# New instruction orders for a fused linear-attention and mixture-of-experts kernel: loads, first-batch slots, attention steps, GpSimd sums, layer-2 products

## Chip, cores, metric

The kernel runs on one core of one Trainium2 chip. The metric is the device time of one execution in microseconds (us). Each experiment was timed in five rounds beside the kernel before, on one of three chips, so runs are compared by their ratio to the kernel before of the same call. Traces are one execution each.

## The reference

Linear attention over 8 batches (8 heads, 576 tokens, head size 64) gives rows of 512 numbers. Four experts, each two layers without routing, work on every row and are summed with normalised weights:

```python
def phi(x):
    return np.where(x > 0, x, np.exp(x) - 1.0) + 1.0
q_p, k_p = phi(q), phi(k)
kv = np.einsum('bhsd,bhse->bhde', k_p, v)
z = np.sum(k_p, axis=2)
out = np.einsum('bhsd,bhde->bhse', q_p, kv) / (np.einsum('bhsd,bhd->bhs', q_p, z)[..., None] + 1e-06)
# rows x: (4608, 512); 4 experts, w1: (512, 1024), w2: (1024, 512)
for e in range(E):
    h = np.maximum(x @ w1[e], 0.0)
    y += p[:, e:e + 1] * (h @ w2[e])
```

## The kernel before

The rows are worked on in nine batches of 512 (the ninth collects 64 left-over rows of each of the eight). From the second batch on, both layers use a seven-product scheme in place of eight: half-size blocks P1 to P7, with sums of weights (DVE, once), of tokens (GpSimd) and of h (GpSimd) prepared ahead. One batch with one expert is a *unit*, 14 slots long; 32 units make up most of the time.

Everything hangs on order. Each piece of work is put at a position (a number), all pieces are sorted by position, and each engine then gets its instructions in that order:

```python
work.sort(key=lambda w: w[0:2])
for _, _, g in work:
    g[0](*g[1:])
```

Waits between engines follow from the data and the buffers and are set by the framework. So a position cannot make the result wrong; it decides what an engine stands behind. These are the parts (cuts marked with `...`):

```python
    def layer2_product(j, e, hT, hss, p, i):
        ...
            run, side = pys[i][:, 0:DH], pys[i][:, DH:Dm]    # two halves of one tile in PSUM
        ...
        for k in range(FH):
            nc.tensor.matmul(out=ps, lhsT=lhsT(k), rhs=rhs[:, k], ...)   # L666
        ...
        add_acc(j, e, ns, ps, ds, first and e == 0)          # DVE reads the half (L568); ACT if it is the first and e == 0

    class Block:                      # layer 1 of one unit, half of the rows of h
        # at +0 p1, +3 p2, +5 p6, +8 p7, +9 p5, +9.1 c22, +11 p4, +13 p3
        def p3(self):
            x = xT_of(self.j)
            self.products(self.e5, lambda k: s_block(self.e, 2, k), x[:, 2:4, NH:NT])   # L731
            add_relu(self.h[:, :, 0, NH:NT], self.e5, self.u2)                          # DVE, L715

        ...
            order = L2ORD ...         # (2, 5, 1, 6, 3, 7, 4)
            for m in range(14):
                put_at(at + L2AT[m], layer2_product, j, e, h, hss, order[m // 2], m % 2)
```

P1, P6, P7 and P4 of layer 2 run through the same PSUM half (`run`), one after the other, and DVE adds the half to the output after each. P6 can't start before DVE has read what P1 left.

`DMA` in the configuration is the order in which GpSimd issues the loads of the weights (`w210`: layer 2, expert 1, first half) and of batch 1's parts (`k0`, `v1`, `lk0`). `L2P`, `WS1`, `WS2`, `TS0`, `L1P`, `BLK` and the first `ATTN` entry place the work of the first batch, during which everything is loaded; the second `ATTN` entry, `HSUM`, `L2AT`, `TSUM` place the work of every later batch.

## Time and profile before

| | before |
|---|---|
| time, median of 4 rounds | 507.53 us (506.90 to 507.89) |
| span of the profiled run | 507.7 us |
| first layer-1 matmul of the experts | 18.63 us |
| last matmul, then tail | 502.2 us, then 5.5 us |
| bare stream time of all 4,343 matmuls (columns / 2.4 ns, the slope measured below) | 464.5 us |

From the page of the profile (section 1: busy time by engine; section 2: busy tenths and granted TensorE clock in 40 slices of 12.7 us; section 4: the chain that ended last, by engine):

```profile
span 507.7 us, 11592 instructions
PE 489.3 (96%) x4343; PEld 409.3 (81%) x4343; DVE 377.4 (74%) x800; ACT 337.4 (66%) x680; POOL 357.9 (70%) x339
...
PE   8987989999999999999999999999999999999995
PEld 3445656688888888888888888888888888888884
...
PEclk9999989999999999999999999999999999999999
DMA  8999952653345234442345234523231020002002
...
PE 81%; DMA 7%; DVE 3%; ACT 3%; issue 2%; SPq 1%; POOL 1%; DVEq 0%; POOLq 0%
```

For holes this text uses a finer reading. In this trace a matmul of 256 columns is followed by the next start after 109 ns, one of 512 columns after 216 ns, one of 130 columns after 57 ns (medians); eight of 256 columns take 0.87 us. Columns / 2.4 ns + 2.5 ns, a fit to these medians, gives all three and is taken for every matmul; what passes beyond that is a *hole*. Summed in this way (worked out from the trace's starts):

| stretch, us | 18.4 to 60 | 60 to 80 | 80 to 100 | 100 to 130 | 130 to 480 |
|---|---|---|---|---|---|
| holes before, us | 6.63 | 5.03 | 1.89 | 0.87 | 4.91 |

What TensorE waited for between 18 and 100 us (the waits view, longest in total first: us, times, longest):

```profile
PE py L577 <- DMA w<-in_moe_w_dram: 1.9, 1, 1.9
PE pb L731 <- ACT u L742: 1.9, 4, 0.9
PE pe L731 <- DMA w<-in_moe_w_dram: 1.0, 1, 1.0
PE pb L731 <- DVE s L605: 0.8, 1, 0.8
```

The timeline of TensorE at these loads (start, length, ..., in brackets the idle time before it and its releaser):

```profile
29.66 1.89 PE L577 MATMUL py<-w,h 128*128 128x512 f16 x8 [1.89 <-DMA w<-in_moe_w_dram]
...
43.49 0.61 PE L731 MATMUL pe<-xT,w 128*128 128x256 f16 x4 [0.99 <-DMA w<-in_moe_w_dram]
44.94 0.61 PE L731 MATMUL pb<-tt,s 128*128 128x256 f16 x4 [0.84 <-DVE s L605]
```

The first waits for half of expert 0's w2, the second for half of expert 2's w1, the third for a sum of that w1.

The timeline at the start of a later batch, P1 (`py<-w,h`), a product of layer 1, P1's second half, then P6 (`py<-t,hs`):

```profile
298.00 0.60 PE L666 MATMUL py<-w,h 128*128 128x256 f16 x4
298.44 0.60 PE L731 MATMUL pb<-xT,w 128*128 128x256 f16 x4
298.87 0.60 PE L666 MATMUL py<-w,h 128*128 128x256 f16 x4
299.69 0.60 PE L666 MATMUL py<-t,hs 128*128 128x256 f16 x4 [0.22 <-DVE acc L568]
```

From 298.87 to 299.69 are 0.82 us where 0.44 are needed: a hole of 0.38 us. The bracket says 0.22, because the profile models a matmul's end some 0.16 us past the next possible start (groups follow each other after 0.44 us and are shown 0.60 long). Between 130 and 480 us it shows of before:

```profile
PE py L666 <- DVE acc L568: 1.1, 5, 0.2
PE psum_nd L463 <- DMA qT<-qp: 0.3, 1, 0.3
```

### The profile page before, as it was taken

Reading aid. Unit: us, or ns where it says so; the run is one execution under the profiler, and the core shown is the slowest. Engines: PE = TensorE matmul, PEld = TensorE weight load, DVE = VectorE, ACT = ScalarE, POOL = GpSimd, SP = SyncE. Lnnn points to the kernel's source line nnn. Section 1 sums busy time; section 2 is a strip of 40 time slices with the busy share of each in tenths; the row PEclk is TensorE's granted clock in tenths of the full one; section 3 lists DMA queues with packets and bytes.
Section 4 is the critical chain, followed back from the end, with each engine's and each line's share of the span. In section 5 each row is a group of like instructions: output and inputs, shape, how many; then the busy total and the mean of one; then the engine's idle time right before and its main releaser. Section 6 shows DMA issues by size and latency. Waiting matters only on the chain.

```text
span 507.7 us, 11592 instructions
## 1 busy us (share of the span) xinstructions
PE 489.3 (96%) x4343; PEld 409.3 (81%) x4343; DVE 377.4 (74%) x800; ACT 337.4 (66%) x680; POOL 357.9 (70%) x339
## 2 busy tenths in 40 slices
PE   8987989999999999999999999999999999999995
PEld 3445656688888888888888888888888888888884
DVE  5546878879876987688868886878688756775675
ACT  5756968984889478946895689558954465446530
POOL 4744304687967796779777977697669877987773
PEclk9999989999999999999999999999999999999999
DMA  8999952653345234442345234523231020002002
GB/s 242 199 225 218 281 137 81 222 119 66 99 135 150 65 81 145 149 87 79 125 146 109 60 125 151 113 48 107 84 67 33 8 95 1 1 1 85 1 1 84
DMA packets 81880, 53.65 MB, mean 106 GB/s; under 512 B 46176, under 2 KB 75360, under 8 KB 81824
## 3 DMA queue, kind: packets, MB, share of 16 engines
q1 hardware_dynamic: 71520, 41.12, 28.7%
q0 software_dynamic: 9824, 11.27, 11.9%
q8 instruction: 34, 0.56, 0.4%
q10 hardware_dynamic: 480, 0.52, 0.3%
q14 instruction: 22, 0.18, 0.1%
HBM read 45.16 MB, written 9.44 MB: 108 GB/s over the span
## 4 chain that ended last, share of the span: by engine, by line
PE 81%; DMA 7%; DVE 3%; ACT 3%; issue 2%; SPq 1%; POOL 1%; DVEq 0%; POOLq 0%
PE py L666 36%; PE pb L731 22%; PE pe L731 16%; DMA w<-in_moe_w_dram 5%; PE py L577 3%; DVE acc L568 2%; PE psum_nd L463 1%; DMA rawb<-in_k_dram 1%; DMA qT<-qp 1%; PE psum_kv L423 1%; SPq L274 1%; ACT psum_ee L314 1%; PE pe L666 1%; SPq L252 1%; PE pb L666 0%
## 5 line engine op out<-in xcount | busy, mean ns | idle before, releaser
L568 DVE SCALAR_TENSOR_TENSOR acc<-py,p_sb,acc 128x256 f32<-128x256 f32 (+1 forms) x382 | 180.4, 488 | 53.0 <-PE py L666 47.1
L715 DVE CUSTOM_DVE_ANT_0 h<-pe,u 128x512 f16<-128x512 f32 x140 | 96.5, 689 | 44.0 <-PE pe L731 24.4
L731 PEld LDWEIGHTS <-w 128*128 128x128 f16 x1120 | 108.3, 98 | 21.8 <-issue 3.4
L633 POOL TENSOR_TENSOR hs<-h 128x512 f16<-128x512 f16 x64 | 73.8, 1153 | 65.1 <-DVE h L715 57.3
L666 PEld LDWEIGHTS <-h 128*128 128x128 f16 x1024 | 100.2, 98 | 13.3 <-issue 1.3
L666 PE MATMUL py<-w,h 128*128 128x256 f16 x744 | 106.4, 273 | 0.1
L742 ACT COPY u<-pb 128x512 f32<-128x512 f32 x140 | 82.4, 589 | 34.4 <-PE pb L731 32.4
L731 PEld LDWEIGHTS <-s 128*128 128x128 f16 x840 | 82.2, 98 | 13.4 <-DVE s L605 1.5
L635 POOL TENSOR_TENSOR hs<-hs,h 128x512 f16<-128x512 f16 x64 | 74.7, 1167 | 18.6 <-PE py L666 16.0
L731 PE MATMUL pb<-tt,w 128*128 128x256 f16 x560 | 84.0, 273 | 1.9 <-ACT u L742 1.9
L666 PEld LDWEIGHTS <-hs 128*128 128x128 f16 x768 | 73.8, 97 | 13.4 <-issue 3.1
L639 POOL TENSOR_TENSOR hs<-h,hs 128x512 f16<-128x512 f16 x64 | 74.4, 1162 | 6.4 <-PE py L666 5.4
L666 PE MATMUL py<-t,hs 128*128 128x256 f16 x496 | 74.3, 272 | 1.7 <-DVE acc L568 1.7
L637 POOL TENSOR_TENSOR h<-h 128x512 f16<-128x512 f16 x64 | 74.4, 1162 | 0.0
L757 ACT ACTIVATE h<-pe 128x512 f16<-128x512 f32 x70 | 41.7, 596 | 49.1 <-PE pe L731 47.9
L751 ACT COPY pe<-pb 128x512 f32<-128x512 f32 x70 | 40.6, 580 | 46.8 <-PE pb L731 45.2
L775 ACT ACTIVATE h<-pb 128x512 f16<-128x512 f32 x70 | 41.6, 595 | 3.5 <-PE pb L731 3.2
L731 PE MATMUL pb<-tt,s 128*128 128x256 f16 x280 | 42.0, 273 | 1.0 <-DVE s L605 0.8
L731 PE MATMUL pe<-tt,s 128*128 128x256 f16 x280 | 42.5, 275 | 0.0
L731 PE MATMUL pe<-xT,w 128*128 128x256 f16 x248 | 37.2, 273 | 1.0 <-DMA w<-in_moe_w_dram 1.0
L731 PE MATMUL pb<-xT,w 128*128 128x256 f16 x248 | 37.2, 272 | 0.4 <-ACT h L775 0.3
L577 PE MATMUL py<-w,h 128*128 128x512 f16 x128 | 35.0, 384 | 2.3 <-DMA w<-in_moe_w_dram 1.9
(120 smaller groups left out, 607.9 us busy)
## 6 DMA issues: line engine op xcount, KB each, us to landing
out_dram<-acc SPq DMA_DIRECT2D x32, 256.0 KB, 2.5
w<-in_moe_w_dram POOLq DMA_DIRECT2D x14, 512.0 KB, 10.8
rawb<-in_v_dram SPq DMA_DIRECT2D x26, 256.0 KB, 2.7
rawb<-in_q_dram SPq DMA_DIRECT2D x26, 256.0 KB, 2.9
rawb<-in_k_dram SPq DMA_DIRECT2D x26, 256.0 KB, 2.8
w<-in_moe_w_dram POOLq DMA_DIRECT2D x4, 256.0 KB, 7.5
rawb<-in_k_dram POOLq DMA_DIRECT2D x4, 256.0 KB, 10.6
rl<-in_q_dram SPq DMA_DIRECT2D x16, 64.0 KB, 2.4
```

The lines of the kernel that those rows point to most:

```text
L568: nc.vector.scalar_tensor_tensor(out=acc, in0=ps, scalar=pscal, in1=acc, op0=AO.mult, op1=AO.add)
L577: nc.tensor.matmul(out=py, lhsT=rows(hT, fj)[:, ns * P : (ns + 1) * P], rhs=w2_sb[e][:, fj, :], start=(fj == 0), stop=(fj == FC - 1),)
L633: nc.gpsimd.tensor_tensor(out=hs[0], in0=a21, in1=a22, op=AO.add)
L635: nc.gpsimd.tensor_tensor(out=hs[1], in0=hs[0], in1=a11, op=AO.subtract)
L637: nc.gpsimd.tensor_tensor(out=a21, in0=a11, in1=a21, op=AO.subtract)
L639: nc.gpsimd.tensor_tensor(out=hs[3], in0=a12, in1=hs[1], op=AO.subtract)
L666: nc.tensor.matmul(out=ps, lhsT=lhsT(k), rhs=rhs[:, k], start=first and k == 0, stop=k == FH - 1, skip_group_check=True,)
L715: nc.vector._custom_dve(TENSOR_ADD_SAT, out=out, in0=ps, in1=u, s0=BIG, s1=0.0)
L731: nc.tensor.matmul(out=ps[:, kk], lhsT=lk(kc), rhs=rhs[:, kc], start=first and kk == 0 and kc == 0, stop=kc == 1, skip_group_check=True,)
L742: nc.scalar.copy(u, self.b)
L757: nc.scalar.activation(self.h[:, :, 0, 0:NH], self.e5, AF.Relu)
L775: nc.scalar.activation(self.h[:, :, 1, 0:NH], self.b, AF.Relu)
```

## The change

Its intent: a new order on every engine, so that weights come when they are needed, batch 1's attention holds TensorE up less, and DVE and GpSimd finish before TensorE needs them. No instruction is added or removed. The core of the diff (long lines cut with `...`; `L1P`, `L2P`, `TS0`, `WS1`, `WS2`, `TSUM1`, `PR` and the first `ATTN` entry change in the same way):

```diff
-    "DMA": (..., 'w200', 'w110', 'w201', 'w111', 'w211', 'lk1', 'lv1', 'lk0', 'k0', 'lv0', 'w210', 'w120', 'w121', 'w221', 'v0', 'w220', 'v1', 'k1', 'w130', 'w131', ...),
+    "DMA": (..., 'w201', 'w200', 'w110', 'w111', 'lk1', 'w120', 'lk0', 'w210', 'w121', 'v1', 'w211', 'v0', 'k0', 'w130', 'lv1', 'w131', 'k1', 'k2', 'v2', 'lv0', ...),
-    "BLK": (-4.0, 3.0, 13.0, 20.0, 28.0, 35.0, 53.0),
+    "BLK": (0.5, 7.5, 16.0, 23.0, 31.0, 38.0, 56.0),
 ...
         dict(
-            v=(0.2, 6.3, 8.4, 9.7),
-            k=(1.3, 2.7, 5.7, 11.5),
-            kd=(7.1, 4.3, 10.8, 15.3),
-            lv=13.3,
+            v=(4.4, 8.7, 12.1, 14.8),
+            k=(0.3, 2.9, 6.7, 11.25),
+            kd=(7.1, 3.84, 14.3, 14.8),
+            lv=10.36,
 ...
-    "HSUM": ((-6.3, -5.5, -4.6, -4.4), (1.5, 2.7, 5.4, 7.2)),
+    "HSUM": ((-5.2, -3.9, -3.7, -1.3), (0.3, 2.7, 2.7, 5.7)),
-    "L2AT": (3.7, 3.8, 5.4, 6.6, 7.1, 8.3, 9.0, 10.0, 12.1, 12.5, 13.3, 14.1, 16.5, 16.7),
+    "L2AT": (3.9, 5.0, 5.8, 7.0, 7.2, 8.4, 9.1, 10.3, 12.9, 13.1, 15.1, 15.1, 16.8, 16.8),
-    "TSUM": (-7.4, -1.8, -1.8, 0.0),
+    "TSUM": (-6.7, -4.7, -1.6, -0.7),
```

## The prediction

> **What bounds the kernel now.** 507.37 us. TensorE is the wall: the page gives it 96% busy, the chain of waits 81%. In the timeline eight 256-column matmuls take 0.87 us, 109 ns each[...]. The rest is start (layer 1 begins at 18.6 us), end (last matmul 502.2, then 5.4 us) and holes. From start to start, holes beyond that rate are about 13 us between 18.6 and 100 us and 5 us later: nearly only one of 0.38 us per batch (143, 195, 247, 299, 351 us), layer 2's product waiting for a DVE accumulation, and 0.46 us at 374 us for the transposed q. The change alters orders only, so it can only close or open holes.

> **What moves, costed.**

> 1. Load order. From 15 to 68 us the DMA engines are saturated (share 1.0 to 1.4 in the windows); a weight half lands every 2.5 us, a part of q or k every 0.85, of v 0.67, a left piece 0.3. Before, TensorE waits 2.06 us at 27.4 for half of expert 0's w2 (landed 29.62), and 1.16 and 1.01 us at 42 to 45 for expert 2's w1 (landed 43.44) and its sums. Adding up the new order (estimates): expert 0's w2 complete at 27.1, expert 1's w1 unchanged at 32.05, expert 2's at 40.2, expert 3's at 50.1 (was 55.5), q3 at 62.4. The hole at 27.4 mostly moves: 1.2 us at 31 for expert 1's w1, and 0.6 us because a sum of expert 0 stands before the one needed. The later holes mostly vanish: TensorE is 1.9 us ahead by 43 us.

> 2. Batch 1's attention, 67 to 76 us. Holes of 1.1, 0.8, 0.4 us (ACT copies, DVE norms), then the clock record shows 0.5 from 70.6 to 74.0 us, costing about 1.3 us.[...] New slots spread transposes and norms: about 2 us of holes left, probably no half clock. Gain 2 us.

> 3. Batch 2's steps, 90 to 105 us: waits for ACT (0.5, 0.7, 0.4 us) and DVE; steps later and spread. Gain 1 us.

> 4. Steady state. P6 now follows P1 after 1.3 instead of 0.87 us, which should close each batch's 0.38 us hole; but P4 follows P7 after only 0.87. GpSimd keeps its order except the token sums; its 8.9 us of sums per 12.25 us unit leave slack. Gain 1.5 us net.

> Sum 6.4 us, less 0.5 for new waits: **501.5 us**, 8 in 10 between **496.5 and 506.5**. Faster by over 2% (under 497.2): 0.13; within 2%: 0.85; slower: 0.02.

> **What would show it.** 1: expert 2's w1 landed near 40 us; no TensorE wait over 0.6 us from 36 to 50 us, but one near 31. 2: no half clock after 6 us; holes from 60 to 80 us under 3 us (now 5.4). 3: holes from 90 to 110 us under 1.5 us. 4: no 0.38 us holes at batch starts. TensorE's instructions and DMA bytes equal.

> **What would make it wrong.** Landings not in queue order; ACT or DVE blocked in order by a late part (v3, q2, left v) and holding up copies that TensorE needs; a second half-clock window; P4 waiting in every unit (32 times 0.2 us would eat all of it); or a middle nearly free of holes, which would bring 496.

Two passages are cut that did not rest on this case's traces: in the first paragraph where the rate was taken from and the two totals worked out by it (the fit to the medians above gives 464.5 + 10.9 us for all matmuls), and in step 2 the ground given for the half clock. The forecast's sum keeps its four terms, 1.9 + 2 + 1 + 1.5 = 6.4 us, and came to 507.4 - 5.9 = 501.5 us. But that the half clock would go, 1.3 of step 2's 2 us, was my estimate.

## More of the kernel before

The window from 130 to 480 us as a whole (busy time by engine, clock, DMA share):

```profile
core 0: us, PE busy (x) PEld busy (x) DVE busy (x) ACT busy (x) POOL busy (x), PEclk, DMA share, GB/s
130.00:480.00 350.00, 348.61 (x3262) 310.32 (x3261) 264.79 (x564) 238.51 (x481) 276.55 (x251) 1.00 0.30 85
```

## The result, and the profile after

| | before | after |
|---|---|---|
| time, median of 4 rounds | 507.53 us | 499.81 us (499.19 to 500.12) |
| ratio, 95% interval | | 0.9848 (0.9831 to 0.9865) |
| mean granted clock of the rounds | 0.990 to 1.000 (42 rounds) | 0.998 to 1.000 (4 rounds) |

A ratio is the mean time of one kernel's fast runs over that of the other's of the same rounds, so not quite the ratio of the medians quoted. The change is 1.5% faster, 7.7 us; the prediction was 501.5 us, in a range of 496.5 to 506.5.

The page after:

```profile
span 498.2 us, 11603 instructions
PE 483.7 (97%) x4343; PEld 408.5 (82%) x4343; DVE 378.1 (76%) x800; ACT 337.3 (68%) x680; POOL 357.5 (72%) x339
...
PE   8989989899999999999999999999999999999995
PEld 3546756789898989898989898989898888888884
...
PEclk9999999999999999999999999999999999999999
DMA  8999974642454234632454245523231020002002
...
PE 83%; ACT 6%; DVE 4%; DMA 3%; POOL 1%; issue 1%; POOLq 0%; SPq 0%; ACTq 0%; DVEq 0%
```

Same matmuls, same work: each engine's count is the same (the 11 more of the first line are not counted to any of them). The dip of the clock is gone (granted clock 1.00 from 18 to 60 and from 60 to 100 us) and the weight-load row alternates 8 and 9 where it was a constant 8. DMA falls from 7% to 3% of the chain. The waits of TensorE between 18 and 100 us:

```profile
PE pe L731 <- DMA w<-in_moe_w_dram: 1.0, 1, 1.0
PE pe L731 <- DVE h L715: 0.9, 1, 0.9
PE psum_xl L402 <- DVE kp L321: 0.8, 1, 0.8
```

One load is waited for, not two; two new waits for DVE stand behind it. The timeline at the loads:

```profile
31.24 0.61 PE L731 MATMUL pe<-xT,w 128*128 128x256 f16 x4 [0.97 <-DMA w<-in_moe_w_dram]
31.68 1.46 PE L577 MATMUL py<-w,h 128*128 128x512 f16 x6
33.57 0.61 PE L731 MATMUL pb<-tt,s 128*128 128x256 f16 x4 [0.43 <-DVE s L605]
```

Those are the two holes that the prediction put there, 1.2 and 0.6 us; from start to start they are 1.14 and 0.60 us. The start of the same later batch:

```profile
291.14 0.60 PE L666 MATMUL py<-w,h 128*128 128x256 f16 x4
291.57 0.60 PE L731 MATMUL pb<-xT,w 128*128 128x256 f16 x4
292.01 0.60 PE L666 MATMUL py<-w,h 128*128 128x256 f16 x4
292.44 0.60 PE L731 MATMUL pb<-tt,w 128*128 128x256 f16 x4
292.88 0.60 PE L666 MATMUL py<-t,hs 128*128 128x256 f16 x4
```

P7 of layer 1 now stands between P1 and P6, and nothing waits. The window from 130 to 480 us:

```profile
130.00:480.00 350.00, 349.53 (x3301) 314.18 (x3299) 268.18 (x570) 239.50 (x480) 278.62 (x251) 1.00 0.32 84
```

PE busy hardly moves (348.6 to 349.5). PEld rises from 310.3 to 314.2, 1.2%, and with it the matmuls done in 350 us, from 3,262 to 3,301. In these two lines the weight-load time moves with the matmuls done, and the matmul time (0.3% up) does not.

| holes, us | 18.4 to 60 | 60 to 80 | 80 to 100 | 100 to 130 | 130 to 480 |
|---|---|---|---|---|---|
| before | 6.63 | 5.03 | 1.89 | 0.87 | 4.91 |
| after | 4.00 | 3.35 | 2.43 | 0.00 | 0.66 |

The two profiled spans differ by 9.5 us, the medians by 7.7: the profiled run of before (509.5 us as timed) was a slow one of its kind, with a half-clock window. Which part of the change paid what can't be read from one pair of traces; the experiments are for that.

### The profile page after: what moved, and what is told of

Same layout as the page of the kernel before. It is cut to its first block, busy times and chain, and to the rows that moved or that the text cites. A ratio compares the mean times of both kernels' runs of the same rounds, so it can differ in the third digit from the quotient of the medians.

```text
span 498.2 us, 11603 instructions
## 1 busy us (share of the span) xinstructions
PE 483.7 (97%) x4343; PEld 408.5 (82%) x4343; DVE 378.1 (76%) x800; ACT 337.3 (68%) x680; POOL 357.5 (72%) x339
## 4 chain that ended last, share of the span: by engine, by line
PE 83%; ACT 6%; DVE 4%; DMA 3%; POOL 1%; issue 1%; POOLq 0%; SPq 0%; ACTq 0%; DVEq 0%
PE py L666 37%; PE pb L731 23%; PE pe L731 17%; DMA w<-in_moe_w_dram 3%; PE py L577 2%; PE psum_kv L423 1%; PE psum_nd L463 1%; DMA rawh<-in_k_dram 1%; ACT u L742 1%; ACT vp L330 1%; ACT psum_ee L314 1%; DVE t L622 1%; DVE h L715 1%; DVE acc L568 1%; ACT h L757 1%
## 5 line engine op out<-in xcount | busy, mean ns | idle before, releaser
L568 DVE SCALAR_TENSOR_TENSOR acc<-py,p_sb,acc 128x256 f32<-128x256 f32 (+1 forms) x382 | 182.6, 488 | 46.4 <-PE py L666 40.1
L731 PEld LDWEIGHTS <-w 128*128 128x128 f16 x1120 | 108.6, 98 | 18.4 <-DMA w<-in_moe_w_dram 2.0
L742 ACT COPY u<-pb 128x512 f32<-128x512 f32 x140 | 82.7, 591 | 27.5 <-PE pb L731 26.3
L751 ACT COPY pe<-pb 128x512 f32<-128x512 f32 x70 | 40.2, 574 | 41.4 <-PE pb L731 14.8
L731 PE MATMUL pe<-xT,s 128*128 128x256 f16 x248 | 37.2, 273 | 0.9 <-DVE h L715 0.9
```

The lines of the kernel that those rows point to most:

```text
L568: nc.vector.scalar_tensor_tensor(out=acc, in0=ps, scalar=pscal, in1=acc, op0=AO.mult, op1=AO.add)
L731: nc.tensor.matmul(out=ps[:, kk], lhsT=lk(kc), rhs=rhs[:, kc], start=first and kk == 0 and kc == 0, stop=kc == 1, skip_group_check=True,)
L742: nc.scalar.copy(u, self.b)
L751: nc.scalar.copy(self.e5, self.b)
```

## Experiments

All are edits of the configuration unless code is shown.

### 1. The load order alone

```diff
-    "DMA": <before's>
+    "DMA": <after's>
```

> The kernel before with only the new load order. Theory (load order pays by itself): the 1.16 and 1.01 us holes at 42 to 45 us go, the one at 27.4 us is mostly moved to 31 to 33 us; gain 2 to 2.5 us, ratio about 0.9955. Rival (the new slots of layer 1 and layer 2 are needed to use the earlier landings, or the old slots now block ACT on late k and v parts): gain under 0.8 us, ratio above 0.9985.

Measured: 506.41 us against 508.69, ratio 0.9958 (0.9940 to 0.9976): 2.1 us. (Gains in us are the ratio's.) Holes from 18.4 to 60 us fell from 6.63 to 4.30. The 1.2 and 1.0 us holes at 42 to 45 us are gone; layer 2 runs through at 27 us, and a hole of 1.1 us (as the profile shows it) stands at 32.75 us, for a weight sum. The theory holds. Traces of before's first-batch code themselves differ by 1.2 us in this stretch (5.7 us in run 4, 6.9 in run 3), so it is the places and the times that show it.

### 2. Load order and all first-batch slots

```diff
+ DMA, BLK, L1P, L2P, TS0, WS1, WS2, ATTN[0], TSUM1, PR of after; the rest of before
```

> The kernel before with the new load order and all new slots of the first batch's work and of batch 1's attention, none of the steady-state ones. Theory: gain 4 to 5 us, ratio about 0.991: 2 to 2.5 us of loads, the rest from the transposes and norms between 60 and 76 us and from no half-clock window; the 0.38 us hole of each later batch stays. Rival (the gain is in the steady state): gain of at most 2.5 us, as much as the load order alone.

Measured: 505.43 us, ratio 0.9932 (0.9916 to 0.9947): 3.5 us. That is less than the theory's 4 to 5 and more than the rival's 2.5; the new first-batch slots add 0.26 points (1.3 us) to the load order, and the two intervals overlap. The trace suggests why so little: holes from 60 to 80 us are 3.35 us here and 3.60 with the load order alone. The profiled 5.03 of before hold a half-clock window; in a trace of the same code without one (run 4) it is 3.77.

### 3. Layer 2's products alone

```diff
-    "L2AT": (3.7, 3.8, 5.4, 6.6, 7.1, 8.3, 9.0, 10.0, 12.1, 12.5, 13.3, 14.1, 16.5, 16.7),
+    "L2AT": (3.9, 5.0, 5.8, 7.0, 7.2, 8.4, 9.1, 10.3, 12.9, 13.1, 15.1, 15.1, 16.8, 16.8),
```

> The kernel before with only the new slots of layer 2's products. Theory: the holes at the batch starts (0.38 us each, seven of them, and part of those near 92 to 105 us) close; gain 2.5 to 3.5 us, ratio about 0.994. Rival (the new batch steps on ACT and DVE, or the new sums on GpSimd, close them): no gain, ratio 0.999 or more, holes still there.

Measured: 505.82 us, ratio 0.9946 (0.9928 to 0.9964): 2.7 us, as the theory had it. But the holes did not just close. From 130 to 480 us they fell only from 4.91 to 3.5 us; in each batch two others are there, 0.24 us before a product right behind layer 1's P3, and 0.36 us like this one, a P6 behind layer 1's P7 that waits for an accumulation of DVE in another unit (so neither is at the P4 that I had named):

```profile
273.09 0.60 PE L731 MATMUL pb<-tt,w 128*128 128x256 f16 x4
273.89 0.60 PE L666 MATMUL py<-t,hs 128*128 128x256 f16 x4 [0.20 <-DVE acc L568]
```

### 4. One number

```diff
-    "L2AT": (3.7, 3.8, 5.4, 6.6, 7.1, 8.3, 9.0, 10.0, ...
+    "L2AT": (3.7, 3.8, 5.4, 6.6, 7.1, 8.3, 9.05, 10.0, ...
```

This swaps the first half of P6 with P7 of the block beside it on TensorE, in every unit, and an accumulation with a copy on ACT where the expert is the first. SP's and GpSimd's orders stay the same.

> The kernel before with one number changed: the first half of product 6 goes behind product 7 of the block beside it, so DVE has 1.3 us instead of 0.87 us after product 1. Theory: this alone closes the 0.38 us hole of each batch start, gain 2 to 2.6 us, ratio about 0.9955. Rival: the hole only moves to the second half of product 6 or to another product, gain under 0.6 us.

Measured: 504.05 us, ratio 0.9911 (0.9894 to 0.9927): **4.5 us from one number**, more than the theory and more than all fourteen new numbers of run 3. The holes from 130 to 480 us fell from 4.91 to 1.98 us. At the start of a batch:

```profile
294.72 0.60 PE L666 MATMUL py<-w,h 128*128 128x256 f16 x4
295.24 0.60 PE L731 MATMUL pb<-tt,w 128*128 128x256 f16 x4
295.67 1.04 PE L666 MATMUL py<-t,hs 128*128 128x256 f16 x8
```

P7 stands between P1 and P6, and P6 starts without a hole (0.08 us stand before P7 instead). Where did more than the five holes of 0.38 us come from? Sorting before's 46 holes of that stretch: five of 0.38 us and one of 0.46 make 2.4 us, and forty of 0.01 to 0.14 us make 2.65 (the sum of 4.91 is 0.1 lower because starts in whole ns round both ways). Of the total, 3.26 us in 34 holes stand before a P5 or P6 (`py<-t,hs`) that waits for a DVE accumulation; in this run five are left there, 0.74 us in all. Nearly every unit had a small one, below what the waits view shows (it lists 1.1 us in 5 waits). Part of the gain is not of this stretch: between the two traces the holes also fell from 0.87 to 0.50 us at 100 to 130 us, from 6.63 to 5.7 at 18 to 60, and from 5.03 to 3.77 at 60 to 80, where before has its half-clock window. The last two lie where the code is the same, and so are differences between executions.

### 5. The later batches' steps and sums without the products

```diff
+ ATTN[1], HSUM, TSUM of after; the rest of before
```

> The kernel before with only the new slots of the later batches' attention steps, of GpSimd's sums of h and of the token sums; layer 2's products stay. Theory (the hole at each batch start is product 6 too close behind product 1, so the steps alone don't close it): gain 1 us or less, ratio 0.998 or above, a hole of 0.2 to 0.4 us per batch still there behind product 1. Rival (the steps that keep DVE busy at the batch start make the hole, and moving them closes it): gain 2 us or more, holes from 130 to 480 us down from 5.5 to under 3.5 us.

Measured: 508.96 us against 508.64, ratio 1.0004 (0.9977 to 1.0032). Holes from 130 to 480 us: 5.07 us, and 3.95 of them before P5 or P6. The rival falls: moving DVE's other work does not close the hole.

### 6. All of the steady state

```diff
+ ATTN[1], HSUM, TSUM, L2AT of after; the rest of before
```

> Both steady-state parts together: new slots of layer 2's products, of the later batches' steps, of the sums. The products alone closed the hole behind product 1 and opened two of 0.24 and 0.37 us per batch behind products 3, 7 and 4. Theory: the new steps close those; holes from 130 to 480 us 1.4 us as in the changed kernel (5.5 before); gain 4 to 5 us, ratio 0.991. Rival (parts simply add): no more than the sum of the two alone.

Measured: 504.05 us, ratio 0.9897 (0.9873 to 0.9922): 5.2 us. From 130 to 480 us no hole is left (0.03 us in all):

```profile
130.00:480.00 350.00, 350.00 (x3306) 314.88 (x3305) 268.36 (x572) 241.85 (x485) 280.88 (x255) 1.00 0.32 85
```

The new products pay 2.7 us, the new steps nothing, both together 5.2: the steps close the holes that the new products leave. The times alone would hardly tell this from a plain sum (0.9946 times 1.0004 against 0.9897, and the two were timed in different calls); the holes decide it: 3.5 and 5.1 us in the runs of one part, none with both. Nor do the times tell these 5.2 us from the 4.5 of the one number of run 4: its interval, 0.9894 to 0.9927, holds 0.9897. That number together with the first batch's new order was not tried. Together with run 2, 0.68 and 1.03 points make 1.71 where the whole change measured 1.52; within the intervals, the two parts add up.

### 7. The changed kernel with the old load order

```diff
-    "DMA": <after's>
+    "DMA": <before's>
```

> The changed kernel with the old load order. Theory: it gives back what the load order alone gained, 2 to 2.5 us, ratio to before about 0.989 (the changed kernel has 0.985), with holes at 27 us and at 40 to 44 us. Rival (the new slots only work with the new order, and old landings block ACT and TensorE): it gives back 4 us or more, ratio 0.993 or above.

Measured: 505.55 us, ratio 0.9932 (0.9909 to 0.9955). It gives back 4.3 us (0.84 points), twice what the load order gained by itself: the rival's figure. TensorE's holes in this trace are 1.74 us at 27 us, 1.91 at 38 and 1.17 at 42 us for weights, then 1.06 and 0.89 us at 57 and 60 us for DVE. The new slots are made for the new landings; the 4.3 us are a difference, with an interval of about 1.5 us to either side (an estimate from the two intervals).

### 8 and 9. Is it the holes at 67 to 70 us that bring the half clock?

In the profile of before, the granted clock is 0.5 from 70.6 to 74.0 us, right behind the holes of 1.1 and 0.8 us that end at 68.9 and 70.5 us. That they bring it was my guess. It doesn't come in every execution: with before's first-batch code it is at 70.6 us in the trace of before and at 45 us in that of run 6 (four matmuls of 512 columns take 1.57 us from start to start, 44.99 to 46.56, where 0.86 is usual), while run 4's trace has a mean clock of 0.999, too near 1 for 3.41 us at 0.5 (0.0034 of the mean).

The test puts 15 matmuls of zeros onto a running sum, nine and six, into the two holes of 1.1 and 0.8 us:

```diff
+    zt = pconst.tile([P, 32], FP16, tag="zt", name="zt")
+    nc.vector.memset(zt, 0.0)
+        def fill(n):
+            for _ in range(n):
+                nc.tensor.matmul(out=pys[1][:, 0:256], lhsT=identh, rhs=zt..., start=False, stop=False, ...)
+        put_at(42.9, fill, 9)
+        put_at(43.35, fill, 6)
```

> The kernel before with 15 matmuls of zeros (256 columns, added onto a running sum, so the result stays right) put into the two holes of 1.1 and 0.8 us at 67 to 70 us, where TensorE waits anyway. Theory: they keep TensorE busy, so that no half-clock window of 3.4 us follows; mean clock 0.998 or above in all rounds (before: 0.990 to 1.0, mostly 0.995), gain 0.6 to 1.0 us, ratio 0.9985. Rival: the window has another cause, the clock stays as before and the time too, or is longer by up to 0.3 us.

Measured: 511.36 us against 508.64, ratio 1.0045 (1.0020 to 1.0070). It was slower, and its trace had late loads (the weights of 512 KB landed 11.4 us after their issue, median, against 10.8) and a granted clock of 0.96 between 15 and 60 us, where before has 1.00. The zero tile stood in front and moved other buffers by 64 bytes, so this run tests two things (whether the 64 bytes made the loads late stays open: the two runs' intervals overlap). The second run has the tile in a pool of its own behind all others:

> The fill test again: in the first one the zero tile stood in front of all others and moved every buffer by 64 bytes, and the loads of 15 to 70 us came up to 1.7 us later, so it tested two things. Now the tile stands behind all other buffers. Theory: loads land as before; no half-clock window follows at 70 us; mean clock 0.998 or above in most rounds; gain 0.5 to 1.0 us, ratio 0.9985. Rival ([...]the window has another cause): clock and time as before, ratio 1.000 to 1.001.

Measured: 509.66 us against 508.54, ratio 1.0030 (1.0014 to 1.0046). Loads land as before (the gaps between landings are those of before within 0.1 us, but for the first weights). The two holes are gone (60 to 80 us: 2.0 us of holes), no half-clock window follows in the trace (mean clock 1.000), and the rounds' mean clock is 0.9977, 0.997 to 1.000, against 0.9963, 0.993 to 0.999. And yet it is 1.1 us slower by the medians, 1.5 by the ratio. The zeros take 1.6 us where 1.9 were idle, so they can't have cost that by themselves; in the trace the lead is waited for at 112 us, where the transposed q of batch 2 lands 6.3 us after its issue and TensorE waits 1.4 us. My expectation on the time is wrong. The one on the clock (0.998 or above in most rounds) was met in two rounds of six, and the mean clock is a poor witness: it also counts a stretch of granted clock 0.5 after the last matmul, 0.25 us up to the end of the span in before (from 507.49 us) and 1.19 us in after (from 496.99 us), which takes 0.0002 and 0.0012 from it. Whether filling pays in another place stays open.

The heading's question stays open. In before's trace the 3.41 us ahead of the window have 2.17 us of holes, the longest 1.11 us. But 2.06 us of holes in the 3.41 us from 26.26 us and 2.19 in those from 41.66 us, in the same trace, and 2.19 us in those from 67.62 us in after's, are followed by a granted clock of 1.0. So the sum of the holes alone does not decide; what else does is left open. Run 9 filled the two holes and its trace has no window, but run 4's, with the two unfilled, has none either. That after's trace has none before 496.99 us is one execution, and so does not show that the change keeps it away.

What the half clock costs can be put in two ways. Between 60 and 80 us before's trace has 1.26 us more holes than run 4's. And over the 42 rounds of before, each less its call's mean, time falls by 0.26 us for each 0.001 more of mean clock (correlation -0.77). A window of 3.41 us at half clock takes 0.0034 from the mean clock (half of 3.41 / 508): an estimate of 0.9 us per window. The mean clock went from 0.9956 (the rounds of before in runs 1 to 4) to 0.9988: some 0.8 us of the change's 7.7 go with the clock, a rough estimate, since the stretch after the last matmul is in both means.

### 10 and 11. Mending the holes that are left

After has 1.14 and 0.60 us at 30 to 33 us. One weight sum and one token sum go ahead of the DVE instruction that waits for the load, and ten parts of layer 2 get earlier positions:

```diff
-    "TS0": (-45.9, -40.65, -16.35, 4.5),
+    "TS0": (-45.9, -40.65, -24.6, 4.5),
-    "WS1": ((-13.4, ...
+    "WS1": ((-24.5, ...
-    "L2P": ((..., 0.8, 3.5, 4.5, 4.5, 5.14, 15.0, 19.25, 21.5, 22.15, 23.0, 24.5),
+    "L2P": ((..., 0.8, 3.3, 3.4, 3.42, 3.44, 3.52, 3.54, 8.0, 15.0, 19.25, 23.0),
```

> The changed kernel with the stretch from 28 to 40 us mended: one weight sum of expert 0 and one token sum go ahead of the weight sum that waits for expert 1's second half, and layer 2's parts of expert 0 are moved ahead to fill the wait. Theory: the 1.14 and 0.60 us holes shrink to under 0.6 together, gain 1.0 to 1.5 us over the changed kernel, ratio to before about 0.9825. Rival (TensorE then only waits for the next landing, near 39 us, or for ACT): gain under 0.4 us, ratio 0.984 or above.

Measured: 500.27 us, ratio 0.9845 (0.9828 to 0.9863), as the change itself. The holes at 30 to 33 us are closed, and in their place the waits view from 18 to 60 us has:

```profile
PE py L577 <- ACT acc L566: 1.6, 1, 1.6
PE py L577 <- DMA w<-in_moe_w_dram: 1.0, 1, 1.0
```

TensorE came early to the next load and to an accumulation on ACT. The rival holds.

The next run adds the three more mends that its expectation lists. One is of after's 1.10 us hole at 97.5 us. This is DVE in after, then GpSimd at the same time:

```profile
93.03 0.68 DVE L624 TENSOR_TENSOR w<-w 128x1024 f16<-128x1024 f16 x1
95.05 3.01 DVE L622 TENSOR_TENSOR t<-w,t 128x1024 f16<-128x1024 f16 x2
97.98 0.68 DVE L715 CUSTOM_DVE_ANT_0 h<-pe,u 128x512 f16<-128x512 f32 x1
```

```profile
93.19 1.53 POOL L633 TENSOR_TENSOR hs<-h 128x512 f16<-128x512 f16 x1 [1.45 <-DVE h L715]
94.80 1.16 POOL L635 TENSOR_TENSOR hs<-hs,h 128x512 f16<-128x512 f16 x1
95.92 1.60 POOL L637 TENSOR_TENSOR h<-h 128x512 f16<-128x512 f16 x1
97.48 1.60 POOL L639 TENSOR_TENSOR hs<-h,hs 128x512 f16<-128x512 f16 x1
```

Of the trace's 32 sums of 128x1024, the 26 that overlap no GpSimd instruction (issues of loads aside) take 0.68 to 0.69 us. The sum at 93.03 began before GpSimd's at 93.19: it takes 0.68 us, GpSimd's 1.53, where 1.15 is the median of those that overlap none of these sums. The two at 95.05 began while GpSimd was at work and take 1.45 and 1.64 us, and GpSimd's at 95.92 and 97.48, begun while they ran, 1.60 each. TensorE then waits for the `h` at 97.98. That the overlap makes them longer is read from these times; why it should was not shown.

```diff
-            xl=70.5,
+            xl=73.3,
-    "WS2": (..., (51.4, 64.3, 78.88, 76.35), (64.1, 65.8, 78.95, 80.05)),
+    "WS2": (..., (51.4, 64.3, 66.9, 76.35), (64.1, 65.8, 85.0, 92.0)),
-    "L2P": (..., (..., 45.8, 46.2, 46.25, 47.65, 48.9, 50.1, 51.5, 52.6, 57.65, 58.6), ...
+    "L2P": (..., (..., 45.7, 45.75, 46.25, 46.3, 46.95, 47.2, 47.4, 47.9, 51.6, 52.1), ...
```

> The changed kernel with that, and with layer 2's parts of expert 2 put between the transposes and norms of 64 to 71 us, the left transpose moved behind the sums of k that it waited for (1.01 us hole at 87 us), and three weight sums moved out of the stretch at 95 us where two of them took 3.0 us beside GpSimd and made a 1.10 us hole. Theory: holes from 60 to 100 us fall from 5.9 to under 3 us, gain 3.5 to 4.5 us over the changed kernel, ratio to before about 0.977. Rival (the holes move to the work taken away from later slots): gain no larger than of the first mend alone.

Measured: 500.43 us, ratio 0.9847 (0.9830 to 0.9863). Nothing again. The two holes of 1.0 and 1.1 us went, and others came at 71 us (0.74), 81 us (0.86) and 88 us (0.80): holes from 60 to 100 us are 5.9 us, as in after. That layer 2's parts, moved ahead, had been filling those is the likely reason; no run tests it.

### 12. Mending the front all the way

Here the causes of run 10's two new waits are mended too: the parts that need the late half go back, the accumulation goes ahead of batch 1's `k0` on ACT, and `k0`, the left v and `v3` go back.

```diff
 as run 10, but the last of expert 0's parts at 20.2, and
-    (21.15, 21.2, 21.2, 22.5, 23.75, ...
+    (21.15, 21.2, 23.2, 24.2, 23.75, ...
-            v=(26.0, 28.9, 31.7, 35.5),
-            k=(19.5, 29.8, 32.3, 33.5),
-            lv=29.8,
-            kv=(37.0, 37.3),
+            v=(26.0, 28.9, 31.7, 36.2),
+            k=(22.6, 29.8, 32.3, 33.5),
+            lv=34.8,
+            kv=(37.0, 38.2),
```

> The first mend gained nothing: its trace has new holes of 1.15 us at 42 us (layer 2 of expert 1 waits for the second half of its w2, landed after) and 1.76 us at 45 us (a product waits for an accumulation on ACT that stands behind batch 1's k0, which had not landed). Here those two are mended as well: the parts that need that half go two slots back, the last part of expert 0 goes ahead of k0, k0, the left v and v3 go back on ACT. Theory (ACT's order around late parts and one late half kept the gain away): TensorE is 1 to 1.8 us ahead by 60 us, ratio to before 0.9815 to 0.983, better than the changed kernel's 0.985. Rival (the loads bound this stretch: whatever is gained at 31 us is waited for again at a later landing or in the chain at 64 to 71 us): ratio 0.984 or above, the layer-1 start to 64 us stretch as long as before the mend.

Measured: 499.47 us against 507.35, ratio 0.9843 (0.9815 to 0.9871). The interval holds both theories, and the change's own 0.9848. In the trace TensorE has no hole above 0.43 us up to 53 us. But at 53 and 56 us it waits 0.90, 0.33 and 1.17 us, for DVE and for the left v on ACT that I had moved back. From the first layer-1 matmul to the first small layer-2 product it is 75.3 us against after's 76.0. A gain of 0.6 us is what the trace would allow; the times neither show nor exclude it. No version here is shown to beat the change.

## Why the prediction was right

The range held and the middle was 1.7 us too high. The terms of its sum were less good than their total, and that errors in them cancelled is luck:

| step | predicted gain | measured |
|---|---|---|
| 1. load order | 1.9 us | 2.1 us (run 1) |
| 2. slots of batch 1 | 2 us | 1.3 us (run 2 less run 1), unclear by its interval |
| 3. batch 2's steps | 1 us | nothing seen (see below); their slots are the later batches', so they are in run 6 |
| 4. steady state | 1.5 us net | 5.2 us (run 6, step 3 included) |
| new waits | -0.5 us | in the above |

**Step 1 was right in mechanism and place.** In after's trace the landings follow queue order and add up: expert 0's w2 landed at 26.3 us (predicted 27.1), expert 1's w1 at 31.2 (32.05), expert 2's at 39.1 (40.2), expert 3's at 49.1 (50.1), q3 at 61.4 (62.4); all 0.8 to 1.1 us early; in that run the first weights landed 0.9 us sooner already (16.41 us against 17.34), although they were issued 0.3 us later. Why is open. The two holes named in advance came out at 1.14 and 0.60 us. From 36 to 50 us the longest wait is 0.42 us, as predicted. What was missed is that the slots depend on it: taking the order away later costs 4.3 us (run 7).

**Step 2 failed.** "Holes of 1.1, 0.8, 0.4 us" were to shrink to 2 us; after has 3.35 us between 60 and 80 us, and the test "under 3 us" failed. A trace of the old code without a half-clock window has 3.77 us, so the slots moved holes and removed few. The half-clock window did vanish in the trace, but with the old code too it comes in some executions and not in others (runs 8 and 9: at 70.6 us, at 45 us, not at all). The estimate of 1.3 us for it was of the right size for one trace (1.26 us there, 0.9 by the rounds), but counting it as always there was wrong.

**Step 3 failed as put.** Its path was wrong: with batch 2's new steps and the old load order (runs 5, 6 and 7) the holes from 90 to 110 us are 2.5, 2.5 and 2.3 us, as in before (2.5); with the new load order alone (run 1) they are 1.3. Over all traces they are 1.6 to 2.5 us with the old order and 1.3 or less with the new: it is the load order that closes them, and what that pays is in step 1's. In after, holes from 90 to 110 us fell to 1.26 us, under the 1.5 that I had named, but a new one of 1.01 us at 87 us and one of 1.10 at 97.5 us made 80 to 100 us worse, 2.43 us against 1.89.

**Step 4 was mis-sized, by up to 3.7 us.** The sentence "nearly only one of 0.38 us per batch" is the step that failed. I had listed holes from 0.15 us up, and forty smaller ones made more than half of the 4.9 us between 130 and 480 us. The sum of "5 us later" stood in the same paragraph and did not fit with six holes of 0.4. The mechanism named, P6 too close behind P1, is shown by run 4: one number gave 4.5 us. The worry that other products would wait in their place was right for the products alone (run 3, 3.5 us of holes left), though not at P4, and wrong for the whole, because the new steps and sums remove those (run 6; which of them was not tested).

The errors were of opposite sign, some 1.7 us too much in the first batches and up to 3.7 too little later, and so the total came out near.

## What to carry to other kernels

Measure a pipelined engine from start to start and sum all of it before listing the big pieces: forty holes that no waits view shows outweighed the six that one sees. Where two engines hand one buffer half to and fro, one more independent piece of work between the writes, in every repetition, may be worth more than many clever moves elsewhere. In a stretch that waits for loads and short chains, a closed hole tends to open further on: mend it and look at where the next wait ends before counting the gain.
